# Radix-4 forward transforms, staggered convolution steps, transposed gate and up, and convolution loads on the POOL queue: one change to a training-step kernel of a gated convolution and a bilinear unit

## The chip, the cores and the metric

The kernel runs on one core of one Trainium2 chip. Its time is the device time of one execution in microseconds (us). In the profiles PE is TensorE's matmuls, PEld its weight loads, DVE VectorE, ACT ScalarE, POOL GpSimd and SP SyncE. A name such as L60 is a line of the kernel whose profile it is. SPq and POOLq are an engine's DMA queue.

A ratio below is the mean time of one kernel's fast runs over that of the other's fast runs of the same rounds. It is therefore not quite the ratio of the medians quoted beside it. Brackets after a ratio are its 95% interval.

## The reference, cut to what matters

The function has S = 2048 positions, D = 1024 channels and F = 3584 hidden units. The kernel returns the output and nine gradients.

```python
def _A_ref(q, k, v, shift_k, ssm_k, ssm_D):           # the convolution branch
    k_shift = sum(k_pad[:, t:t + S, :] * shift_k[:, 3 - t] for t in range(4))   # 4 taps
    kv = k_shift * v
    # long convolution of kv with ssm_k: FFT of length 2S, product, inverse FFT
    y = irfft(rfft(kv_pad) * rfft(kf_pad))[:, :S]
    return q * (y + kv * ssm_D)

def _B_ref(x, w_gate, w_up, w_down):                  # the bilinear branch
    return ((x @ w_gate) * (x @ w_up)) @ w_down

xn = layernorm(A_q)
out = A_q + _A_ref(xn, k, v, ...) * silu(_B_ref(xn, ...))
# reference(): out and the vjp for q, k, v, shift_k, ssm_k, ssm_D, w_gate, w_up, w_down
```

## The kernel before

The program has four stages, and TensorE works in all of them.

1. **Forward:** layer norm, tables, gate/up (matmul tile `psg`) with the forward convolution woven in.
2. **Down:** the down projection (`psbm`) and the elementwise work of both branches.
3. **Back:** dh and dw of gate and up (`psdh`, `psdw`), then dw_down (`psdw` again), with the backward convolution and the gradient dk woven in.
4. **dx** (`psx`).

The convolution is a generator. A "pump" advances it after each unit of matmul work. In these traces each engine takes its instructions in program order, and so does each DMA queue. The timelines below show it: VectorE stands 43.01 us for `k` while TensorE waits 43.09 us for another result of VectorE. All loads go through `ld` (the SP queue) and all stores through `st` (the POOL queue).

The sequence is laid out so that partition u holds rows 8u to 8u+7 of one half c. The four-tap shift needs three earlier rows as well. So partition u loads rows 8u-3 to 8u+7, which is eleven rows. For c = 0, partition 0 has no earlier rows. It is loaded apart, and the main load covers partitions 1 to 127.

```python
def ld(out, in_):
    return nc.sync.dma_start(out=out, in_=in_)
def st(out, in_):
    return nc.gpsimd.dma_start(out=out, in_=in_)
# ... forward convolution, per group of 256 channels and half c:
                k = kst.tile([P, 11, 256], BF16, name="k")
                if c == 0:
                    V.memset(k[0:1, 0:3, :], 0.0)
                    ld(k[0:1, 3:11, :], kin[0:8, d0:d0 + 256].rearrange("(o r) d -> o r d", o=1))
                    ld(k[1:P, :, :], bass.AP(kin.tensor, kin.offset + 5 * D + d0, [[8 * D, P - 1], [D, 11], [1, 256]]))
                else:
                    ld(k[:], bass.AP(kin.tensor, kin.offset + 1021 * D + d0, [[8 * D, P], [D, 11], [1, 256]]))
                v = kst.tile([P, 8, 256], BF16, name="v")
                ld(v[:], vin[:, c, :, d0:d0 + 256])
                # ... VectorE: shift, kv; st(KSHd), st(KVd) ...
# ... the forward transform, radix 8 (fwd_unit): matmuls psS and psP per r, then on VectorE
            nc.scalar.copy(out=s, in_=psS[:])
            tt(W[:, n * h:n * h + n, :], s, psP[:], ADD)
            tt(W[:, 8 + n * h:8 + n * h + n, :], s, psP[:], SUB)
            yield 1.25 * nr
        dft_even(W, 0, W[:, 16:20, :], X, False)
        yield 5.2
        dft_odd(W, 8, W[:, 16:18, :], X, False)
        yield 7.0
# ... the gradient dk, per group of 128 channels, loads at the head of the unit:
        ld(kh[1:P, 0, :, :], bass.AP(kin.tensor, kin.offset + 5 * D + d0, [[8 * D, P - 1], [D, 11], [1, P]]))
        ld(kh[:, 1, :, :], bass.AP(kin.tensor, kin.offset + 1021 * D + d0, [[8 * D, P], [D, 11], [1, P]]))
        ld(dk[:, :, 0:8, :], src)
        ld(dk[0:P - 1, :, 8:11, :], src[1:P, :, 0:3, :])
        # ... VectorE products into acc, then
            st(o_dk[:, c, :, dsl], acc[:, c])
# ... dw_down, the stage that dk is woven into:
                wb = bg.tile([P, 512], BF16, name="wb")          # two buffers
                nc.scalar.copy(out=wb[:], in_=ps[:])
                st(o_dwd[f0:f0 + P, dh * 512:(dh + 1) * 512], wb[:])
```

## Time and profile before

| | before |
|---|---|
| median (three runs) | 2803.95 us (2802.9 to 2810.16) |
| granted TensorE clock, mean | 0.927 |
| PE / DVE / POOL busy | 79% / 55% / 21% |
| stage lengths in the profiled run: forward, down, back, dx | 777, 332, 1260, 433 us |

The stage lengths are read from the tile view, which gives the first and last start of each tile's matmuls. "Forward" runs from the start to the first `psbm`, "down" to the first `psdh`, "back" to the first `psx`.

These lines of the page of before give busy time and share per engine, then the span in 40 equal slices. Each digit is a busy share in tenths, and PEclk is the clock granted to TensorE in tenths of full speed.

```profile
PE 2217.0 (79%) x14506; PEld 1222.7 (44%) x14506; DVE 1545.0 (55%) x2273; ACT 870.6 (31%) x1141; POOL 587.7 (21%) x972
...
PE   0739859598738995899999998889876553999998
...
PEclk9979989799968997999999999999997786999999
```

TensorE is the limiting engine, with dips. There is one in the third slice, some over the forward stage, and a long one near the end (slices 30 to 34), which is dw_down. The PEclk digits dip with them.

The timeline of before has start, length, engine, line and operation. In brackets it gives the idle time before an instruction and what ended it. The lines are from the SP queue, VectorE and TensorE.

```profile
7.49 35.51 SPq L57 DMA_DIRECT2D v<-in_A_v_dram  x1
...
157.70 40.19 SPq L57 DMA_DIRECT2D v<-in_A_v_dram  x1
...
2052.45 23.63 SPq L57 DMA_DIRECT2D kh<-in_A_k_dram  x3
...
202.68 1.23 DVE L161 TENSOR_TENSOR acc<-k,Wbc 128x2048 bf16<-128x2048 bf16 x1 [43.01 <-DMA k<-in_A_k_dram]
...
211.13 1.86 PE L217 MATMUL psP<-hx,TF 128*128 128x128 bf16 x16 [43.09 <-DVE W L161]
```

The issue of `v` stands 35 to 40 us on the SP queue, directly behind a `k` load for c = 0. VectorE then waits 43 us for `k`, and TensorE 43 us for VectorE.

The windows view of before has one row per stretch: busy us of each engine with its instruction count, granted clock, mean share of the 16 DMA engines, and GB/s.

```profile
180.00:190.00 10.00, 0.00 (x0) 0.00 (x0) 0.00 (x0) 0.00 (x0) 0.00 (x0) 0.50 0.07 20
110.00:800.00 690.00, 535.11 (x3880) 297.46 (x3879) 538.08 (x739) 264.19 (x381) 140.25 (x255) 0.90 0.51 175
1945.00:2310.00 365.00, 245.71 (x1088) 109.29 (x1086) 137.35 (x230) 63.88 (x69) 42.20 (x71) 0.87 0.38 108
```

The first row lies inside that hole. No engine works, and the DMA share is 0.07 at 20 GB/s. The share is the mean over 16 DMA engines, and one of sixteen is 0.0625: by this estimate one DMA engine is moving data and fifteen stand.

The waits view of before, 1945 to 2370 us, gives who waited for what: total us, times, longest.

```profile
DVE dka L161 <- DMA dkh<-DKSHd: 215.7, 8, 30.4
...
POOL out_dram L60 <- DVE dka L161: 161.3, 16, 33.2
...
PE psY L718 <- DMA dkh<-DKSHd: 110.4, 7, 33.2
ACT wb L796 <- DMA out_dram<-wb: 100.8, 20, 19.7
```

In dw_down VectorE waits for the loads of dk. The stores of dk on the POOL queue wait for VectorE. The stores of `wb` stand behind them, and ScalarE gets no free `wb` buffer to empty TensorE's accumulators into.

### The profile page before, as it was taken

To read this page: it belongs to the slowest core of one execution; us is meant where nothing else is said; L and a number is where in the kernel's file an instruction comes from. 1 tells how busy PE (TensorE), PEld (TensorE's weight loads), DVE (VectorE), ACT (ScalarE), POOL (GpSimd) and SP (SyncE) were. 2 spreads that over 40 slices of the span, in tenths; PEclk is the share of its full clock that TensorE was granted. 3 is DMA by queue.
4 is the path that set the end of the run, shared out by engine and by line. 5 is a ranking of instruction groups with operands and counts; after the bars stand their busy time and mean duration, and the time that the engine had idled before them with its cause. 6 is when DMAs were issued, how large, how long until landed. Compare 5 with 4: busy or idle time off the path is not lost. (4 is left out here: it accounts for less than half of the span.)

```text
span 2802.4 us, 36132 instructions
## 1 busy us (share of the span) xinstructions
PE 2217.0 (79%) x14506; PEld 1222.7 (44%) x14506; DVE 1545.0 (55%) x2273; ACT 870.6 (31%) x1141; POOL 587.7 (21%) x972
## 2 busy tenths in 40 slices
PE   0739859598738995899999998889876553999998
PEld 0325435255424443565566555554432221544443
DVE  3639959599984695457556654655542233132222
ACT  1634324244302222444334433553320000221111
POOL 0103212122202331234333433223110110000000
PEclk9979989799968997999999999999997786999999
DMA  3426544445546997547556654436543336443330
GB/s 103 154 89 214 182 154 174 168 175 203 184 175 227 354 318 206 166 151 224 176 170 204 219 160 145 157 132 215 162 116 90 82 84 200 137 179 124 124 124 23
DMA packets 277068, 465.35 MB, mean 166 GB/s; under 512 B 79398, under 2 KB 200226, under 8 KB 263459
## 3 DMA queue, kind: packets, MB, share of 16 engines
q1 hardware_dynamic: 219236, 273.19, 31.3%
q0 software_dynamic: 57664, 189.86, 18.8%
q8 instruction: 113, 1.85, 0.3%
q14 instruction: 55, 0.45, 0.1%
HBM read 273.15 MB, written 189.80 MB: 165 GB/s over the span
## 5 line engine op out<-in xcount | busy, mean ns | idle before, releaser
L369 PE MATMUL psg<-wslab,XNT 128*128 128x512 bf16 x1792 | 421.3, 385 | 3.2 <-ACT gu L371 3.2
L630 PE MATMUL psdw<-dgu,XN 128*128 128x512 bf16 x1792 | 405.0, 380 | 9.4 <-DVE dgu L161 8.2
L161 DVE TENSOR_TENSOR W<-W 128x512 f32<-128x512 f32 (+1 forms) x384 | 315.5, 822 | 7.3
L845 PEld LDWEIGHTS <-dgut 128*128 128x128 bf16 x1792 | 174.5, 98 | 207.0 <-DMA dgut<-DGUTd 0.8
L630 PEld LDWEIGHTS <-XN 128*128 128x128 bf16 x1792 | 172.1, 98 | 198.5 <-issue 11.4
L369 PEld LDWEIGHTS <-XNT 128*128 128x128 bf16 x1792 | 172.1, 99 | 186.1 <-issue 13.6
L60 POOL DMA_DIRECT2D out_dram<-wb x280 | 155.3, 572 | 378.0 <-ACT wb L634 207.7
L793 PE MATMUL psdw<-DBMT,dgu 128*128 128x512 bf16 x896 | 204.7, 386 | 22.4 <-ACT wb L796 15.0
L609 PE MATMUL psdh<-wdt,DBMT 128*128 128x256 bf16 x1792 | 217.1, 274 | 1.0 <-ACT DBMT L598 0.9
L509 PE MATMUL psbm<-wd,ht 128*128 128x512 bf16 x896 | 201.4, 383 | 6.9 <-ACT bm L511 2.6
L60 POOL DMA_DIRECT2D DGUTd<-gt x224 | 155.1, 754 | 239.6 <-ACT gt L621 227.6
L371 ACT CAST gu<-psg 128x512 bf16<-128x512 f32 x224 | 130.8, 586 | 237.5 <-PE psg L369 205.8
L609 PEld LDWEIGHTS <-DBMT 128*128 128x128 bf16 x1792 | 171.2, 98 | 20.9 <-ACT DBMT L598 2.0
L161 DVE TENSOR_TENSOR W<-W,psP 128x1024 f32<-128x1024 f32 (+1 forms) x112 | 115.1, 1064 | 102.6 <-PE psP L217 54.2
L845 PE MATMUL psx<-WGU,dgut 128*128 128x512 bf16 x768 | 169.3, 379 | 0.0
L793 PEld LDWEIGHTS <-dgu 128*128 128x128 bf16 x896 | 88.5, 99 | 130.5 <-issue 23.5
L621 ACT COPY gt<-tr 128x1024 bf16<-128x1024 bf16 x112 | 114.4, 1021 | 85.9 <-PE tr L620 68.0
L634 ACT CAST wb<-psdw 128x512 bf16<-128x512 f32 x112 | 66.0, 589 | 240.7 <-PE psdw L630 224.0
L161 DVE TENSOR_TENSOR m<-A,B 128x1024 bf16<-128x1024 bf16 x128 | 82.5, 686 | 105.5 <-DMA B<-KFd 84.4
L509 PEld LDWEIGHTS <-ht 128*128 128x128 bf16 x896 | 87.3, 99 | 109.3 <-issue 9.2
L161 DVE TENSOR_TENSOR dxn<-psx,dxna_t 128x1024 f32<-128x1024 f32 x16 | 19.6, 1225 | 206.6 <-PE psx L845 206.4
L217 PEld LDWEIGHTS <-TF 128*128 128x128 bf16 x1536 | 97.4, 101 | 79.5 <-issue 64.1
(193 smaller groups left out, 2946.9 us busy)
## 6 DMA issues: line engine op xcount, KB each, us to landing
GUd<-gu POOLq DMA_DIRECT2D x56, 512.0 KB, 3.0
ht<-HTd SPq DMA_DIRECT2D x16, 1792.0 KB
gul<-GUd SPq DMA_DIRECT2D x56, 512.0 KB
DGUTd<-gt POOLq DMA_DIRECT2D x224, 128.0 KB, 5.0
dgut<-DGUTd SPq DMA_DIRECT2D x16, 1792.0 KB
A<-DYFd SPq DMA_DIRECT2D x16, 1024.0 KB
Hd<-h POOLq DMA_DIRECT2D x56, 256.0 KB, 3.9
HTd<-hT POOLq DMA_DIRECT2D x112, 128.0 KB, 4.0
```

The lines of the kernel that those rows point to most:

```text
L60: return nc.gpsimd.dma_start(out=out, in_=in_)
L161: V.tensor_tensor(o, a, b, op)
L217: nc.tensor.matmul(ps[:, 2 * i + k, g * P:(g + 1) * P], TF[:, r0 + i, c, k, g * P:(g + 1) * P], x[:, 8 * c + r0 + i, :], start=(c == 0), s ...
L369: nc.tensor.matmul(ps[:], XNT[q][:, dc, i * P:(i + 1) * P], w[:, dc].rearrange("p a f -> p (a f)"), start=(dc == 0), stop=(dc == DC - 1))
L371: nc.scalar.copy(out=gu[:, i].rearrange("p a f -> p (a f)"), in_=ps[:])
L509: nc.tensor.matmul(ps[:], ht[:, fc, i * P:(i + 1) * P], wds[fc // 4][:, fc % 4, :], start=(fc == 0), stop=(fc == NF - 1))
L609: nc.tensor.matmul(ps[:, i, :], DBMT[:, dc, b * P:(b + 1) * P], wdt[:, dc, :], start=(dc == 0), stop=(dc == DC - 1))
L621: nc.scalar.copy(out=gt[:, 2 * pp:2 * pp + 2], in_=ps[:])
L630: nc.tensor.matmul(ps[:].rearrange("p a f -> p (a f)"), XN[:, b, dc * P:(dc + 1) * P], dgus[b // 4][:, b % 4].rearrange("p a f -> p (a f)" ...
L634: nc.scalar.copy(out=wb[:], in_=ps[:])
L793: nc.tensor.matmul(ps[:], hs[b // 4][:, b % 4, fi // 2, (fi % 2) * P:(fi % 2 + 1) * P], DBM[:, b, dh * 512:(dh + 1) * 512], start=(b == 0) ...
L845: nc.tensor.matmul(ps[:, dh * 512:(dh + 1) * 512], t[:, a, 4 * j + f, :], WGU[j][:, a, f, dh * 512:(dh + 1) * 512], start=(j == 0 and a == ...
```

## The change

Its intent is to take work off VectorE, which was 78% busy in the forward stage and takes its instructions in order. It also shortens the convolution's steps so that they disturb TensorE less, and takes the convolution's loads out of the SP queue, where they stood ahead of the weight loads. The core of the diff, cut:

```diff
+    cld = st                                    # convolution loads: the POOL queue
+    def cld_k(t, c, d0, w):
+        if c == 0:
+            nc.vector.memset(t[0:1, 0:3, :], 0.0)
+            cld(t[0:1, 3:11, :], kin[0:8, d0:d0 + w].rearrange("(o r) d -> o r d", o=1))
+        p0 = 1 - c
+        for (a, b) in ((0, 6), (6, 11)):
+            off = kin.offset + (1021 * c + 5 * (1 - c) + a) * D + d0
+            cld(t[p0:P, a:b, :], bass.AP(kin.tensor, off, [[8 * D, P - p0], [D, b - a], [1, w]]))
 ...
-    GUd = dram.tile([NSL, P, NB, 2 * SLW], BF16, name="GUd")
+    GUTd = dram.tile([NF, P, 2, S], BF16, name="GUTd")      # gate and up kept transposed
 ...
+    def fwd4(x, X, wp, psp):                    # radix 4: half of the butterflies by matmul
+        for par, T in ((0, TF), (1, TFO)):      # a second table, TFO
+            W = wp.tile([P, 12, 256], F32, name="W")
+            for i in range(2):
+                ...
+                cmm(psS, T, x, (i, i + 4))
+                cmm(psP, T, x, (i + 2, i + 6))
+                nc.scalar.copy(out=s, in_=psS[:])
+                yield 0.1
+                tt(W[:, 2 * i:2 * i + 2, :], s, psP[:], ADD)
+                tt(W[:, 4 + 2 * i:6 + 2 * i, :], s, psP[:], SUB)
+                yield 1.4
+            dft4(W[:, 0:4, :], W[:, 4:8, :], X, par, False)
+            yield 2.8
 ...
+    def staggered(main, tail, lag):             # the end of one unit inside the next
+        n = 0
+        for w in main:
+            yield w
+            n += 1
+            if tail is not None and n > lag:
+                w = next(tail, None)
+                ...
 ...
+    def gu_unit(fc, qs, w, tick):               # gate/up: weights stationary, 512 positions move
+                    nc.tensor.matmul(ps[:], w[:, dc, a, fi * P:(fi + 1) * P], XNT[q][:, dc, :], ...)
 ...
-                    nc.tensor.matmul(ps[:, i, :], DBMT[:, dc, b * P:(b + 1) * P], wdt[:, dc, :], ...)   # dh, 256 columns
+                nc.tensor.matmul(ps[:], wdt[:, dc, fi * P:(fi + 1) * P], DBMT[:, dc, s0:s0 + 512], ...) # dh, 512 columns
 ...
+    def dk_load(ds, ew):                        # loads of dk one unit ahead, double-buffered
+        for c in range(2):
+            cld_k(kh[:, c], c, ds * P, P)
+        ...
+            cld(dk[:, c], bass.AP(src.tensor, src.offset + 1024 * c * P, [[8 * P, P], [P, 11], [1, P]]))
```

There is more. The layer norm is cut into smaller pieces, the integer products of the tables are made by POOL instead of VectorE, and the first weight slabs load through the ScalarE queue. The backward transforms (`fwd8`) and inverse transforms are cut into steps of 2 to 3 us, and the whole backward convolution is one generator, of which 7% is pumped in down and the rest evenly over back. DKSHd gets eight zero rows, so the `dk` load becomes a full 128-partition load. The `k` and `kh` loads of c = 0 stay at 127 partitions.

## The prediction

> **What bounds it now.** The groups view gives a matmul with 512 columns in a full stream 0.215 us and one with 128 columns 0.056 us. Counting all matmuls at these rates, TensorE needs about 2085 us of 2804; about 720 us are stalls. The stage table (windows view) places them:
>
> - start to the first gate/up matmul: about 67 us. The first vector sum waits until 55 us: the convolution's k and v loads stand ahead of x on the SP queue, and one issue there is held 35.5 us.
> - gate/up plus forward convolution (to about 785 us): 500 us of matmul, about 210 lost. VectorE is 78% busy and in order; the waits view has 71 us for k loads plus 28, one a 43 us hole on TensorE at 167-211 us.
> - down projection (to 1077): about 70 lost, half of it draining the forward convolution.
> - dh/dw with backward convolution (to 1945): about 140 lost, much of it VectorE in lumps of 8 to 17 us, plus A/B loads.
> - dw_down (to 2366): about 210 lost. VectorE waits 216 us for dkh; one kh issue holds the SP queue 22-25 us; the dk stores wait on the POOL queue (161 us), so wb is not freed and TensorE stops.
> - dx: about 25 lost.
>
> [...] The trace shows the long hold, not yet the POOL case.
>
> **What changes.**
> - Radix-4: a forward transform on VectorE goes from about 17.5 us (4x1.22 + 2x1.22 + 10x0.69 + 8x0.42) to 16x0.684 = 10.9 us; 16 of these: about -105 us of VectorE. TensorE gains 1024 matmuls of 128: +57 us. That stage becomes TensorE-bound, VectorE about 455 of 600 us.
> - dh at 512 columns: 1792x0.118 to 896x0.215, about -18 us TensorE. Gate/up had 512 already; transposes stay 896 and 448.
> - POOL issues: DGUT 224 to 56; about 200 convolution loads added: POOL time about equal.
> - New on TensorE: 2140 us in a full stream.
> - Convolution loads leave SP, one unit ahead; dk loads double-buffered; steps of 2-3 us instead of 5-17; backward convolution spread over down, dh/dw and dw_down.
>
> **Sum.** Losses after: start and table build 55 (gate/up matmuls by 35 us); forward stage 50; down 40 (DMA still 78-98% busy); dh/dw and dw_down together 85 instead of 350; dx 30. 2140 + 260 = **2400 us**, 14% less. All of the stall savings are on the critical path, since TensorE is the limiting engine; the 105 us of VectorE count only as far as they remove TensorE's waits, and cost 57.
>
> Range for 8 in 10: 2310 to 2520. Faster by over 2%: 0.96; within 2%: 0.03; slower: 0.01.
>
> **What would show it right.** TensorE over 88% busy in the forward stage, that stage ending near 665 us; no 20 us waits for k or dkh; dh/dw plus dw_down near 1030 us instead of 1290; dx unchanged near 435; granted clock above 0.96; VectorE near 1420 us.
>
> **What would make it wrong.** The POOL queue is now shared by stores and convolution loads, in order: a load waiting for its buffer, or a 127-partition load still on one engine, delays stores behind it, so gut, dgt or wb are not freed and TensorE stops as before. The table build (POOL integer products, single-buffered) may hold the first transforms 20-30 us. Single-buffered W couples ScalarE and VectorE. Then 2500 or more. If stalls nearly vanish, 2280.

What the trace of before shows of such loads on the SP queue is the issue behind them standing 35 to 40 us and a DMA share of 0.07 at 20 GB/s, the estimated one engine of above. "The POOL case" is the same load on the POOL queue, which the trace of before does not hold.

## The result and the profile after

| | before | after |
|---|---|---|
| median (four runs each) | 2803.89 us | 2886.21 us (2879.93 to 2892.62) |
| ratio | 1 | 1.0289 [1.0259, 1.0319], slower |
| granted clock, mean | 0.927 | 0.910 |
| forward, down, back, dx | 777, 332, 1260, 433 us | 909, 277, 1265, 440 us |

The changed kernel is 2.9% slower. Down became 55 us shorter, forward 131 us longer, and back did not move although its matmuls got shorter.

The same lines of the page, after:

```profile
PE 2250.8 (78%) x14369; PEld 1200.7 (42%) x14634; DVE 1446.9 (50%) x1947; ACT 859.1 (30%) x1204; POOL 782.8 (27%) x990
...
PE   0573939859997988599999999999733454899998
...
PEclk9886979979998999799999999999866776999999
```

VectorE lost 98 us as intended. POOL gained 195 us, and the dips are still there: slices 4, 6 and 9 in the forward stage, and a long one in slices 28 to 33, which is dw_down.

The timeline of after around the first of the deep dips, POOL, then VectorE, then TensorE:

```profile
224.76 5.66 POOL L60 DMA_DIRECT2D k<-in_A_k_dram  x1 [1.20 <-issue]
253.01 6.18 POOL L60 DMA_DIRECT2D k<-in_A_k_dram  x1 [22.59 <-issue]
259.18 1.56 POOL L60 DMA_DIRECT2D v<-in_A_v_dram  x2
...
261.28 0.73 POOL L60 DMA_DIRECT2D GUTd<-gut  x1
...
225.72 0.69 DVE L182 TENSOR_TENSOR hT<-gut 128x1024 bf16<-128x1024 bf16 x1 [0.28 <-DMA KSHd<-acc]
278.25 1.23 DVE L182 TENSOR_TENSOR acc<-k,Wbc 128x2048 bf16<-128x2048 bf16 x1 [51.83 <-DMA hrow<-in_A_ssm_k_dram]
...
235.40 1.06 PE L231 MATMUL psS<-kv,TFO 128*128 128x128 bf16 x16
281.86 1.89 PE L231 MATMUL psP<-kv,TFO 128*128 128x128 bf16 x16 [45.41 <-DVE W L182]
```

Read it from the top. POOL spends 5.66 us on issuing one half of the `k` load, then stands 22.59 us, then spends 6.18 us on the other half. The store of `gut` comes only after that. VectorE's next instruction reads `k` and waits 51.83 us. The view names the DMA that landed last by the profile, `hrow`, but the instruction reads `k` and `Wbc`. TensorE waits 45.41 us for VectorE.

In the two later deep dips (slices 6 and 9) the held stores are what stops the engines. The waits view of after, 240 to 886 us:

```profile
DVE HX L182 <- DMA HFd<-HX: 98.6, 6, 45.9
ACT gut L457 <- DMA GUTd<-gut: 84.2, 2, 42.3
```

In the first of them the store of `HX` (the result of a forward transform) is issued at 403.70 us, directly behind half of a `k` load, and VectorE stands 45.55 us until it has landed. ScalarE stands 41.92 us for the store of `gut`, and TensorE 45.69 us in turn. The second repeats this.

The timeline lines above show one thing more: what an idle spell costs afterwards. In their last line sixteen matmuls of 128 columns take 1.89 us where they took 1.06 before. The windows view of after gives the granted clock around them: 1.00 in 238 to 240 us, 0.76 in 240 to 242, 0.50 inside this hole (first row of the view below) and still 0.50 in 281 to 284, when TensorE works again, then 0.82 in 284 to 288 and 1.00 in 288 to 292.

The windows view of after, for that hole, the forward stage, and dw_down:

```profile
242.00:248.00 6.00, 0.00 (x0) 0.00 (x0) 0.00 (x0) 0.00 (x0) 0.00 (x0) 0.50 0.07 20
240.00:886.00 646.00, 488.00 (x4262) 308.19 (x4335) 434.70 (x563) 213.53 (x329) 162.66 (x203) 0.89 0.47 156
1967.00:2450.00 483.00, 252.65 (x1178) 118.77 (x1198) 148.63 (x215) 59.67 (x80) 172.24 (x139) 0.77 0.47 103
```

The hole has the signature that it had before: DMA share 0.07, 20 GB/s. By the same estimate the load runs on one DMA engine on the POOL queue too. POOL's busy time in the last row is 172 us, against 42 in the like row of before.

The waits view of after, 1967 to 2450 us:

```profile
ACT wb L955 <- DMA out_dram<-wb: 284.2, 9, 71.8
DVE dkp L182 <- DMA dkh<-DKSHd: 207.6, 7, 31.6
...
PE psdw L952 <- ACT wb L955: 154.3, 7, 27.5
POOL kh L60 <- issue: 122.0, 14, 14.9
...
DVE dka L182 <- DMA dkh<-DKSHd: 58.4, 1, 58.4
```

The chain is as before, with one link more. The wait of ScalarE for a free `wb` grew from 100.8 to 284.2 us, and TensorE waits 154 us for ScalarE. The `kh` loads now stand in the same in-order queue as the stores of `wb`.

The group of the `kh` issues (issues, busy us, mean ns, idle before) on the page of after:

```profile
L60 POOL DMA_DIRECT2D kh<-in_A_k_dram x40 | 113.0, 2828 | 128.8 <-issue 122.0
```

These 40 issues take 113 us of POOL and are preceded by 129 us of standing. The tile view has 2.8 us, 6.6 us and 27.8 us as the minimum, median and maximum from issue to landing for `k`.

### The profile page after: what moved, and what is told of

Read it like the earlier page. It is cut to its first block, busy times and chain, and to the rows that moved or that the text cites. A ratio compares the mean times of both kernels' runs of the same rounds, so it can differ in the third digit from the quotient of the medians.

```text
span 2890.8 us, 35638 instructions
## 1 busy us (share of the span) xinstructions
PE 2250.8 (78%) x14369; PEld 1200.7 (42%) x14634; DVE 1446.9 (50%) x1947; ACT 859.1 (30%) x1204; POOL 782.8 (27%) x990
## 4 chain that ended last, share of the span: by engine, by line
issue 37%; PE 26%; DMA 13%; DVE 12%; POOL 8%; ACT 3%; POOLq 0%; SPq 0%; DVEq 0%; ACTq 0%
PE psdw L909 9%; DMA kh<-in_A_k_dram 4%; PE psbm L785 4%; DVE W L182 3%; PE psdw L952 3%; PE psdh L891 2%; PE psg L455 2%; POOL kh L60 2%; DMA HFd<-HX 2%; DVE m L182 1%; PE tr L902 1%; POOL out_dram L60 1%; DMA wrow<-DBMd 1%; DVE dgt L182 1%; DMA k<-in_A_k_dram 1%
## 5 line engine op out<-in xcount | busy, mean ns | idle before, releaser
L455 PE MATMUL psg<-XNT,wslab 128*128 128x512 bf16 x1708 | 414.7, 391 | 9.3 <-ACT XNT L442 4.4
L952 PE MATMUL psdw<-DBMT,dgu 128*128 128x512 bf16 x874 | 206.0, 393 | 155.7 <-ACT wb L955 154.3
L455 PEld LDWEIGHTS <-wslab 128*128 128x128 bf16 x1792 | 175.9, 101 | 203.3 <-issue 28.8
L457 ACT CAST gut<-psg 128x512 bf16<-128x512 f32 x224 | 131.1, 586 | 304.6 <-PE psg L455 209.5
L891 PE MATMUL psdh<-DBMT,wdt 128*128 128x512 bf16 x858 | 213.2, 389 | 5.0 <-ACT dht L893 1.4
L182 DVE TENSOR_TENSOR W<-W 128x512 f32<-128x512 f32 (+1 forms) x272 | 213.3, 784 | 7.0
L182 DVE TENSOR_TENSOR W<-W,psP 128x512 f32<-128x512 f32 x192 | 122.3, 682 | 121.4 <-PE psP L231 72.5
L955 ACT CAST wb<-psdw 128x512 bf16<-128x512 f32 x56 | 32.0, 585 | 395.0 <-DMA out_dram<-wb 284.2
L60 POOL DMA_DIRECT2D kh<-in_A_k_dram x40 | 113.0, 2828 | 128.8 <-issue 122.0
L903 ACT COPY dgu<-tr 128x1024 bf16<-128x1024 bf16 x112 | 113.4, 1012 | 103.0 <-PE tr L902 102.4
L468 PE MATMUL tr<-ident,hT 128*128 128x128 bf16 x448 | 36.9, 224 | 124.4 <-DVE hT L182 123.0
L1005 PE MATMUL psx<-XN,dgut 128*128 128x512 bf16 x501 | 116.8, 387 | 16.8 <-DMA dgut<-DGUTd 16.3
```

What stands on the lines that cost most here:

```text
L182: V.tensor_tensor(o, a, b, op)
L455: nc.tensor.matmul(ps[:], w[:, dc, a, fi * P:(fi + 1) * P], XNT[q][:, dc, :], start=(dc == 0), stop=(dc == DC - 1))
L457: nc.scalar.copy(out=gut[:, a, k * 512:(k + 1) * 512], in_=ps[:])
L468: nc.tensor.transpose(ps[:, i, :], hT[:, i * P:(i + 1) * P], ident[:])
L891: nc.tensor.matmul(ps[:], wdt[:, dc, fi * P:(fi + 1) * P], DBMT[:, dc, s0:s0 + 512], start=(dc == 0), stop=(dc == DC - 1))
L903: nc.scalar.copy(out=dgu[:, :, a, fi * P:(fi + 1) * P], in_=ps[:])
```

## The experiments

**Theory A** says that the shape of one load is the cause. A load over 127 partitions runs on one DMA engine on either queue, as estimated above from the DMA share of 0.07 at 20 GB/s, on SP in before and on POOL in after. Put on the POOL queue it also holds that queue (issues of 5.66 and 6.18 us with 22.59 us between them), so the stores behind it come late and buffers are not freed. That other partition counts would do better was the estimate, which e1 and e5 test; why they should is not shown.

**The rivals** put the loss elsewhere: to the move of the loads into a queue that they share with the stores, whatever their shape, or to the new structure (radix-4, small steps, staggering, table build). The texts call theory A by that letter and say what each rival expects.

Runs of one job share the runs of before. Where runs of different jobs are compared, their ratios to before are the fairer measure.

### e1: the changed kernel, 127 partitions cut into 112 and 15

```diff
-        for (a, b) in ((0, 6), (6, 11)):
-            off = kin.offset + (1021 * c + 5 * (1 - c) + a) * D + d0
-            cld(t[p0:P, a:b, :], bass.AP(kin.tensor, off, [[8 * D, P - p0], [D, b - a], [1, w]]))
+        for (pa, pb) in (((1, 113), (113, P)) if c == 0 else ((0, P),)):
+            for (a, b) in ((0, 6), (6, 11)):
+                off = kin.offset + (1021 * c + 5 * (1 - c) + a + 8 * (pa - p0)) * D + d0
+                cld(t[pa:pb, a:b, :], bass.AP(kin.tensor, off, [[8 * D, pb - pa], [D, b - a], [1, w]]))
```

> The changed kernel; each load of k and kh that spans 127 partitions is cut into one of 112 and one of 15 partitions, still on the POOL queue, same bytes. Theory A (a 127-partition load runs on one DMA engine on the POOL queue too, fills it, and holds the in-order POOL queue with all stores behind it): the holes of 45-50 us in the forward stage (three of them) and the 30-45 us per dk unit go, time about 2480 us (2400 to 2560); the POOL issue of such a load falls from 5.6-6.2 us to about 1 us each. Theory B (sharing the POOL queue between loads and stores is what costs, whatever the shape of the load): at most 60 us gained, 2820 or more, since two more loads stand in the queue. Theory C (radix-4 and finer steps cost more than they save): no change, 2880.

Measured: **2480.01 us** (2478.21 to 2484.73), ratio 0.8835 [0.8819, 0.8851], before 2807.32. Nothing changed but the cut of the load, with the same bytes on the same queue in the same order. It took 406 us off the changed kernel. That the median meets the expected 2480 us to the microsecond is luck; the expected range was 2400 to 2560.

Page of e1:

```profile
PE 2240.1 (90%) x14634; PEld 1189.4 (48%) x14634; DVE 1447.3 (58%) x1947; ACT 859.7 (35%) x1204; POOL 675.3 (27%) x1014
...
PE   3779999999979895799999999989998978999997
...
PEclk9889999999989997999999999999999989999999
...
L953 PE MATMUL psdw<-DBMT,dgu 128*128 128x512 bf16 x896 | 199.0, 381 | 0.6 <-ACT wb L956 0.6
```

The long dip of dw_down is gone, and TensorE waits 0.6 us for ScalarE there instead of 154.3. The groups of e1 by form, for the same issues:

```profile
L60 POOL DMA_DIRECT2D kh<-in_A_k_dram x56 | 40.6, 737 | 11.8 <-PE psY L756 10.1 <-issue 1.6
...
L60 POOL DMA_DIRECT2D k<-in_A_k_dram x28 | 20.4, 733 | 8.3 <-DVE prod L183 5.1 <-DVE q L183 3.2
```

There are more issues, but each takes 0.74 us instead of 2.83, and the standing before `kh` falls from 129 us to 12. The longest landing of `k` falls from 27.8 to 11.3 us.

### e2: the cut in the dk stage alone

```diff
+        for (pa, pb) in (((1, 113), (113, P)) if c == 0 and w == P else ((p0, P),)):
```

> As the first, but only the kh loads of the dk units are cut; the forward k loads keep 127 partitions. Theory A: the end of the backward convolution recovers alone, about 250 to 280 us, so 2610 to 2640; the three holes in the forward stage stay. Theory B and C: 2860 to 2890.

Measured: 2667.28 us (2664.78 to 2667.77), ratio 0.9496 [0.948, 0.9513]. This is 27 us above the upper end that A expected, but the direction and the place are right. The `psdw` matmuls of dw_down run from 1963.2 to 2205.3 us, a length of 242 us as in e1 (after: 459). The forward stage keeps its holes, with `psg` from 86.9 to 887.9. So the cut in dk is worth 219 us (2886 to 2667) and the cut in the forward stage 187 us (2667 to 2480).

### e3: the uncut k and kh loads put back on the SP queue

```diff
-            cld(t[0:1, 3:11, :], kin[0:8, d0:d0 + w].rearrange("(o r) d -> o r d", o=1))
+            ld(t[0:1, 3:11, :], kin[0:8, d0:d0 + w].rearrange("(o r) d -> o r d", o=1))
 ...
-            cld(t[p0:P, a:b, :], bass.AP(kin.tensor, off, [[8 * D, P - p0], [D, b - a], [1, w]]))
+            ld(t[p0:P, a:b, :], bass.AP(kin.tensor, off, [[8 * D, P - p0], [D, b - a], [1, w]]))
```

> The changed kernel with only the k and kh loads moved back to the SP queue, uncut (127 partitions). Theory B: the stores are free again, 2400 to 2500. Theory A: the hold moves to the SP queue, where it keeps back weight and gate/up loads instead of stores; the data come as late as before, so some gain from the stores but not most of it: 2650 to 2850, with single SP issues held over 20 us.

Measured: 2716.37 us (2715.23 to 2716.95), ratio 0.9674 [0.9659, 0.9688]. Taking the slow loads out of the queue of the stores gives back 170 of the 406 us. The other 236 us stay, because the loads are still slow. The timeline of e3 has the SP queue held instead:

```profile
207.71 29.01 SPq L57 DMA_DIRECT2D k<-in_A_k_dram  x3
```

So the queue matters, but as the second factor. With good shapes it hardly matters, as e7 shows.

### e4: the kernel before, with its own loads cut

```diff
-                    ld(k[1:P, :, :], bass.AP(kin.tensor, kin.offset + 5 * D + d0, [[8 * D, P - 1], [D, 11], [1, 256]]))
+                    for (pa, pb) in ((1, 113), (113, P)):
+                        ld(k[pa:pb, :, :], bass.AP(kin.tensor, kin.offset + (8 * pa - 3) * D + d0,
+                                                   [[8 * D, pb - pa], [D, 11], [1, 256]]))
 ...  # kh[1:P] the same way; dk[0:P - 1] in (0, 112), (112, P - 1)
```

> The kernel before, with its 127-partition k, kh and dkh loads cut into 112 and 15 (15 or 112 at the end) on the SP queue. Theory A: its own holes (43 us and 28 us in the forward stage, 35 us at the start, about 25 us in each of eight dk units) go: 2804 less 230 to 320, so 2480 to 2570. Theory B: unchanged within 1%, 2780 to 2820.

Measured: **2532.11 us** (2524.74 to 2538.01), ratio 0.9017 [0.8995, 0.9038]. The old kernel had the same fault and gains 275 us from the same cut. This is the comparison that isolates the rest of the change: 2532 to 2480 us, 52 us or 2%.

### e5: the same cut, but into 113 and 14

```diff
-        for (pa, pb) in (((1, 113), (113, P)) if c == 0 else ((0, P),)):
+        for (pa, pb) in (((1, 114), (114, P)) if c == 0 else ((0, P),)):
```

> As the first experiment, but the 127 partitions are cut into 113 and 14 instead of 112 and 15: as many loads, nearly the same sizes. Theory A [...] most of the gain is lost again, 2750 to 2850. Rival A2 (any load is fine once it is short enough, for instance under 700 row pieces): the same as 112 and 15, 2470 to 2500.

Measured: 2825.02 us (2821.37 to 2828.51), ratio 1.0048 [1.0033, 1.0063], before 2811.98 in this job. One partition moved from one piece to the other costs 345 us against e1. There are as many issues as in e1, about as many bytes in each, and the same queue. It is therefore not the size of the load or the number of pieces, but its partition count.

The DMA view, with all its rows, shows this load by load. These are the halves of `k` with six rows: KB each, and median us from issue to landing.

```profile
k<-in_A_k_dram POOLq DMA_DIRECT2D x4, 384.0 KB, 5.6
k<-in_A_k_dram POOLq DMA_DIRECT2D x4, 381.0 KB, 27.4
...
k<-in_A_k_dram POOLq DMA_DIRECT2D x4, 336.0 KB, 5.1
...
k<-in_A_k_dram POOLq DMA_DIRECT2D x4, 339.0 KB, 25.0
```

The first two are the loads of 128 and of 127 partitions in after. The third is that of 112 partitions in e1, the fourth that of 113 in e5. Of the large counts only these four were run: the two that sixteen divides land in 5.6 and 5.1 us, the two that it does not in 27.4 and 25.0 us. How other counts do, and why, is not shown here.

Groups of e5 by form:

```profile
L60 POOL DMA_DIRECT2D kh<-in_A_k_dram x56 | 113.1, 2027 | 105.2 <-issue 99.6 <-DMA kh<-in_A_k_dram 5.7
L60 POOL DMA_DIRECT2D k<-in_A_k_dram x28 | 56.9, 2035 | 91.5 <-issue 83.2 <-DVE prod L183 5.1 <-DVE q L183 3.2
```

The 56 `kh` issues take 113.1 us here and 40.6 us in e1.

### e6: e1 with radix-8 in the forward stage

```diff
-            yield from fwd4(kvs, KX, cs, ps_cv)
+            yield from fwd8(kvs, KX, cs, ps_cv)
-            yield from fwd4(S_["hx"], HX, cs, ps_cv)
+            yield from fwd8(S_["hx"], HX, cs, ps_cv)
 ...  # the second table TFO is neither built nor kept
```

> The first experiment's kernel with the radix-8 forward transform in the first phase (in the new fine steps) and without the second table. VectorE gains about 110 us of work, TensorE loses 1024 matmuls of 128 columns (57 us in a full stream) and the table build is halved. If VectorE bounds the forward stage: 40 to 100 us slower than 2480. If TensorE bounds it, as the prediction said: 20 to 60 us faster, 2420 to 2460.

Measured: 2553.73 us (2553.25 to 2560.46), ratio 0.9089 [0.9074, 0.9103]. Radix-4 is worth 0.0254 of the time of before, about 71 us, in this structure, although it adds matmuls to the limiting engine and a table. The windows view of e6 after its last gate/up matmul shows why:

```profile
690.00:800.00 110.00, 27.30 (x253) 21.93 (x252) 86.56 (x112) 11.26 (x19) 5.43 (x8) 0.58 0.34 122
```

The gate/up matmuls have ended at 691.8 us. VectorE, with its longer transforms, is still busy 87 of 110 us with the rest of the convolution, and TensorE works 27 of them. With radix-4 this gap is 22 us.

### e7: e1 with all convolution loads back on the SP queue

```diff
-    cld = st
+    cld = ld
```

> The first experiment's kernel with every convolution load on the SP queue. If sharing the POOL queue with the stores still costs once the shape is mended: 20 to 80 us faster than 2480. If the POOL queue is right for them, because loads that wait for a buffer would hold weight loads on SP: 20 to 100 us slower.

Measured: 2472.19 us (2467.82 to 2476.81), ratio 0.8793 [0.8778, 0.8808]. It is faster than e1 by 8 us in the medians, 0.0042 in the ratios. The expectation, 20 to 80 us in either direction, missed: with loads of good shape the queue is worth almost nothing. The part of the change that moved the loads to POOL gained nothing.

### e8: e1 without the staggering

```diff
+        if tail is not None:
+            yield from tail
+            tail = None
         for w in main:
 ...
-            if tail is not None and n > lag:
+            if False:
```

> The first experiment's kernel with each unit's inverse rows run before the next unit's steps instead of between them, in both convolutions. If staggering matters: 25 to 70 us slower than 2480, with waits of VectorE for the row copies (yl, yf) doubled from the 56 us of yl; if not, within 10 us.

Measured: 2502.4 us (2498.66 to 2504.89), ratio 0.89 [0.8886, 0.8914]. Staggering is worth 22 us in the medians, 0.0065 in the ratios, which is just under the expected 25 to 70. The wait expected to grow, VectorE's for `yl`, did not. It is 29.4 us without staggering and 55.6 us with it. The gain is real, but the expected reason for it is not confirmed.

### e9b and e10b: tables earlier, and XN on the POOL queue

These were first submitted under labels without the "b". No chip ran those submissions, and the same kernels were sent again.

```diff
 # e9b, against e7
+    build_tables(ps_tr)          # before build_bcast, ahead of the first gate/up units
     build_bcast(ps_y)
 ...
-    build_tables(ps_tr)
 # e10b, against e9b
-                ld(XN[:, 4 * q:4 * q + 4, :], XNd[:, 4 * q:4 * q + 4, :])
+                st(XN[:, 4 * q:4 * q + 4, :], XNd[:, 4 * q:4 * q + 4, :])
```

> The all-on-SP kernel of the seventh experiment with the sine tables built right after the first layer-norm block instead of after the last. Between 100 and 180 us VectorE waits there for the POOL products of the tables and TensorE is at 72 to 85%. If the late tables cost, 15 to 35 us faster than 2472; if the forward stage is bound by TensorE's matmuls alone, under 10 us.

> As the ninth, and the four 1 MB loads of XN go through the POOL queue, so that they no longer stand before the small DBM loads that the first dh products need (one 20 us issue on SP, TensorE at 39% in 960-1000 us). 10 to 20 us faster than the ninth; the best version so far, about 2435.

Measured: e9b 2466.69 us (2465.86 to 2471.39), ratio 0.8797 [0.878, 0.8813]. e10b 2476.29 us (2472.41 to 2480.84), ratio 0.8826 [0.8803, 0.8848], before 2804.51 in both. e9b has the lowest median of all, but its ratio does not differ from that of e7. The first table is ready by about 34 us and the second by about 59, but the convolution is first pumped after the early gate/up units, and the first transform still starts at 184 us. e10b missed: moving the loads of XN made it 10 us slower.

### e11 and e12: the convolution starts earlier, with radix-4 and with radix-8

```diff
 # e11, against e9b: the gate/up units of the last 512 positions come after the layer norm, with ticks
-        for fc in range(4):
-            gu_unit(fc, [q], slabs[fc // 2], nop)
+        if q < 3:
+            for fc in range(4):
+                gu_unit(fc, [q], slabs[fc // 2], nop)
 ...
+    for fc in range(4):
+        gu_unit(fc, [3], slabs[fc // 2], tick)
 # e12: e11 with fwd8 for fwd4, one table
```

> The ninth experiment's kernel (radix-4, loads cut and on SP, tables early) with the forward convolution started with the last layer-norm quarter's gate/up matmuls instead of after them; its first transform comes near 140 us instead of 184. If the late start of the convolution costs (VectorE is half idle from 45 to 200 us there), 15 to 40 us faster than 2467. If the forward stage is held by TensorE's work alone, within 10 us of it.

> As the eleventh with the radix-8 forward transform and one table. In the sixth experiment radix-8 left 106 us between the last gate/up and the first down matmul, because VectorE lagged. If that lag came from the late start, this is 30 to 60 us faster than the sixth (2554), so 2490 to 2525; radix-4 keeps an advantage of 30 to 60 us over it. If the lag is only the amount of VectorE work, it stays near 2540.

Measured, with before at 2808.66 in both: e11 2478.07 us (2472.51 to 2481.77), ratio 0.8828 [0.8805, 0.8851]. e12 2527.04 us (2523.08 to 2531.41), ratio 0.9009 [0.8984, 0.9035]. The first transform starts at 158 us instead of 184, and with radix-4 nothing comes of it: a miss. With radix-8 the time falls 27 us below e6, of which the SP queue may be about 10 (e7), and it ends just above the expected 2490 to 2525. The gap between the last gate/up and the first down matmul stays: 107 us (674.6 to 781.5), against 106 in e6. That fits VectorE's amount of work holding the forward stage with radix-8 and TensorE holding it with radix-4, but it does not prove it. In this pair, on one chip, radix-4 is worth 49 us.

## Why the prediction was wrong

The predicted time was 2400 us (2310 to 2520), and 2886 us was measured. The miss of 486 us has two parts.

**406 us: the step that failed.** It is the step "Convolution loads leave SP, one unit ahead; dk loads double-buffered", costed in the sum as "forward stage 50" and "dh/dw and dw_down together 85 instead of 350". The sum took it that a 127-partition load stops being slow once it is on another queue and issued earlier. The prediction had written the risk down twice ("not yet the POOL case", and "a 127-partition load still on one engine, delays stores behind it"), but gave it no place in the sum and one chance in a hundred of being slower. The runs show the opposite. The load keeps to an estimated one engine on POOL (DMA share 0.07, 20 GB/s), costs POOL 5.7 to 6.2 us to issue, and holds the stores behind it. Cutting it by 112 and 15 takes 406 us off (e1), and cutting it by 113 and 14 takes only 61 off (2886 to 2825, e5).

The data to price the risk stood in the profile of before: 20 GB/s in the hole at 180 us. One half of `k` is 127 x 6 x 256 x 2 bytes, 390 kB. At 20 GB/s that is an estimated 19.5 us, in a queue where a store is due every few us.

**About 80 us: losses set too small.** This table counts TensorE's work in each stage as the prediction did: 0.215 us for a matmul of 512 columns, 0.118 for 256, 0.056 for 128, times their number in e1. The prediction ascribes the rates for 512 and 128 columns to the groups view. They are the distances between starts in the timeline: in after a stream of 15 matmuls of 512 columns took 3.24 us (starts at 232.16 and 235.40), 216 ns each, and 16 of 128 columns took 0.90 us (229.26 to 230.16), 56 ns each. The groups view's mean for 512 columns is 379 to 393 ns, because there neighbours overlap. The 0.118 us is busy time: 15.12 us for 128 `psdh` matmuls in 1330 to 1400 us of before. Inside a stream their starts are 109 ns apart (43 of them in 4.86 us from 1203.62), and at that rate the 512-column dh would save an estimated 3 us and not 19. The loss is the stage's length in the profiled run less that work. For after, whose trace lacks some matmul records, the work of e1 is taken.

| stage | loss predicted | loss in e1 | loss in after |
|---|---|---|---|
| start and forward | 105 | 147 | 335 |
| down | 40 | 58 | 59 |
| back | 85 | 101 | 325 |
| dx | 30 | 30 | 33 |
| sum | 260 | 337 | 751 |

The work itself comes to 2140 us in e1, as predicted, and the loss of dx was right. With the load mended, the sum is short by 77 us, half of it in the start and the forward stage. The last two columns also locate the shape's cost: 188 us in forward and 224 us in back, next to nothing elsewhere. e2 gave 187 and 219 us for the same two places.

**Point by point:**

- *VectorE near 1420 us:* 1447. Right. The costing of radix-4 on VectorE holds.
- *TensorE over 88% busy in the forward stage, ending near 665 us:* 488.00 of 646.00 us, 76%, and 886 us. In e1 it is 96%, and the last `psg` starts at 698.6 us. The windows view of e1 has

```profile
200.00:700.00 500.00, 478.47 (x4272) 298.72 (x4269) 424.12 (x547) 212.04 (x327) 133.26 (x199) 1.00 0.57 194
```

- *No 20 us waits for k or dkh:* wrong, 51.83 us for `k` and up to 58.4 us for `dkh`. Mended, VectorE's waits for `k` sum to 9.7 us, but one wait of 33.0 us for `dkh` remains in e1.
- *dh/dw plus dw_down near 1030 us:* 1241 us in after. In e1 it is 1018 (997.7 to 2015.5).
- *dx near 435 us:* 440.
- *Clock above 0.96:* 0.91. In e1 it is 0.967.
- *POOL about equal:* wrong, 588 to 783 us. With the load mended it is still 675. The prediction set 168 fewer DGUT issues against some 200 new loads, but left out the length of a 127-partition issue (the `kh` issues average 2.83 us in after and 0.74 in e1).

**What the rest of the change is worth.** Both kernels with the same cut, from their profiled runs. In brackets is TensorE's work, counted as above from each kernel's own matmuls, plus the loss.

| stage | e4 (before, cut) | e1 (after, cut) |
|---|---|---|
| forward | 649 us (505 + 145) | 721 us (574 + 147) |
| down | 337 us (228 + 108) | 277 us (218 + 58) |
| back | 1117 us (959 + 158) | 1041 us (940 + 101) |
| dx | 432 us (409 + 23) | 438 us (408 + 30) |

Over the kernel the rest of the change adds 39 us of matmul work and takes away 98 us of loss. Back has 19 us less work by this count, nearly all of it the 512-column dh, and 58 us less loss. Which of the small steps, the loads ahead and the staggering saves these 58 us was not run apart, except that staggering is worth 22 us over the whole kernel (e8). Backward transforms were not moved from down to back to speak of: of the 256 `psS` matmuls on `dyx`, 144 come before the first `psdh` in e4 and 136 in e1.

The forward stage of the new structure is the longer one even without the fault, by 72 us, but its loss is the same. It holds 69 us more matmul work by this count. The 1024 matmuls of radix-4 are 57 us of that, a price that e6 shows to be worth paying in this structure. The other 12 us are 208 matmuls of the forward convolution that the old kernel runs only after its first `psbm`, where they count as down. TensorE waits 38 us for them there, so most of the 50 us that down loses less is this tail. Forward and down together take 986 us in e4 and 998 us in e1.

The old kernel starts its convolution sooner: its first transform begins near 130 us, in e1 near 185. VectorE fills less of the start in e1 (73.09 of 155.00 us in 45 to 200) than in e4:

```profile
43.00:200.00 157.00, 139.10 (x936) 75.15 (x934) 120.17 (x172) 90.70 (x130) 33.03 (x63) 0.95 0.56 196
```

e11 started it sooner and gained nothing with radix-4, which fits the equal losses. What makes up the 147 us that the forward stage still loses is left open. So is the reason why staggering pays its 22 us.

## What to carry to other kernels

Count the partitions of every load: here one over 127, cut into 112 and 15, gave 406 us in one kernel and 275 in the other, and cut into 113 and 14 only 61. Look for a DMA share of 0.07 at 20 GB/s in an idle hole, which was the mark of the slow load here. Before moving a slow load to another queue, ask why it is slow and what will stand behind it there: in dw_down of after, ScalarE waited 284.2 us for late stores to free `wb`, and TensorE 154.3 us for ScalarE. A risk that a prediction names must be priced in its sum, and a change is fairly credited only against a baseline that has had the same fault mended: here that is 52 us and not 324.
